# Clustered attention and MLP: the mix's second product moved from the attention into the MLP, onto gathered, turned tokens

## The chip, the cores and the metric

One NeuronCore of one Trainium2 chip runs the whole kernel. The metric is the device time of one launch in microseconds (us); the time of a version is the median of its runs. All numbers below come from the times of the version before the change and from one profiled execution of it.

## The reference, cut to what matters

The attention has 4 batches, 8 heads, 768 tokens and 64 columns per head. A query may only see keys of its own cluster. Its output, laid out as x with 768 tokens by 512 columns per batch, goes through a mix over tokens of rank 32 and an MLP:

```python
mask = q_assign[:, :, :, None] == k_assign[:, :, None, :]
scores = np.where(mask, scale * np.matmul(q, k.transpose(0, 1, 3, 2)), -1000000000.0)
attn = np.exp(scores - np.max(scores, axis=-1, keepdims=True))
attn = attn / (np.sum(attn, axis=-1, keepdims=True) + 1e-09)
x = np.matmul(attn, v)                      # then (B, S, H * D)

xt = x.transpose(0, 2, 1)
h = xt @ U @ V                              # U is 768x32, V is 32x768
u = x + h.transpose(0, 2, 1)
out = u + np.maximum(u @ w_ch1, 0.0) @ w_ch2
```

The mix of one batch is therefore u = x + Vᵀ(Uᵀx): a first product with U that needs the x of the whole batch, and a second with V, whose result is added to x.

## The kernel before, in words

**Attention.** The heads of a batch are taken in pairs, so there are 16 pairs, four to a batch. A pair goes through `rowmax` (24 matmuls of 384 columns, each followed by a DVE maximum, L421 and L423), `scores` (L445, L447, then an exponential on ACT, L450), `weights` (sums of exponentials, mostly on POOL, L460) and `values` (L468). Ahead of these stand the loads, the split of the inputs into a high and a low part, the choice of clusters on DVE (`clusters`) and several DMAs that put rows in place; `place_clusters` (L407 to L411) copies the clusters' one-hot rows `ohT`, which `rowmax` of that pair needs. `sums` (L480) makes the denominators, and `normalise` (L494 to L506) turns a pair's output back on PE and writes it, scaled, into the batch's tile `xt`: 128 partitions by 6 groups of tokens by 512 columns.

**The mix.** After a batch's last pair `mix_u` (L508) multiplies by U on PE, `mix_sum` (L523) adds the parts into `x3` (96 by 512), and `mix_v` (L531) runs six times per batch: one matmul of `x3` with a slice of `v3` (L535, 512 columns), and a DVE addition of `xt` to its result (L537). For batches 1 and 2 a DVE transpose of 32 by 32 blocks follows (L539), and `store_u` writes the batch in four DMAs (`store_blocks`, L550) to a scratch tensor `u_blk` in DRAM. Batches 0 and 3 go to `u_scr` untransposed; batch 3 is fetched back in halves inside the MLP, turned there (L753) and stored to `u_blk` (`fetch_half`, `turn_blocks`, `store_half`).

**MLP.** Batch 0 goes through two plain products (L596 to L598 and L615 to L617). Batches 1 to 3 use a scheme with seven block products instead of eight: `seven1` (L817 to L819) and `seven2` (L893 to L895), whose results `after1` and `after2` add up on DVE, and `join_up` (L931) joins into the output, after which `store` writes it. Their input is read by `fetch_columns` (L758): 16 DMAs per batch which gather pieces of 128 bytes out of `u_blk`, so that columns lie on partitions, into a tile that the trace calls `f`. `u_sums` (L773) and `u_halves` (L778, L779) work on it from there. The weights of both products go through DRAM too (`wc`); `fetch_w1` (L788) and `fetch_w2` (L800) read them back.

**The order.** Nothing is scheduled by a planner. Every step is put in a list with a time written by hand (`times`, `mixes`, `stages`, and the offsets at the end), the list is sorted, and each engine and each DMA queue runs its steps in that order. In the attention a unit of time is half a score step of a pair, 12 to a pair; in the MLP it is one step of the plain products, 32 for batch 0 and 28 for each of the others, with 24 block matmuls to a unit. Nearly all DMAs are issued by one queue, SP, which waits at the head of its line for whatever the next DMA needs. PSUM gives the work tiles (`work`, L139) four banks.

Of the kernel before, what the change touches and what calls it, by code (L numbers as in the profile page):

```python
# [59 lines left out]
    "load0":           (-34.78, -31.87, -43.69,   None,   None, -25.08),  # L60
    "load1":           (-26.31, -29.08, -32.88,   None,   None, -24.23),
    "sims":            ( -25.34, -28.59, -28.55,   None,   None, -21.62),
    "place_clusters":  (-18.26, -15.82, -15.03,   None, -10.24, -12.43),
    "split_hi0":       (-29.17, -30.78, -24.16,   None,   None, -21.89),
    "split_lo0":       (-23.33, -24.44, -23.58,   None,   None, -17.99),
    "split_hi1":       (-23.81, -23.71, -24.25,   None,   None, -18.05),
    "split_lo1":       (-23.44, -23.17, -23.57,   None,   None, -17.17),
    "place_keys_hi":   (-22.85, -23.61, -22.94,   None,   None, -17.07),
# [10 lines left out]
    "sums":            ( 14.31,  14.69,  13.43,  14.01,  15.60,  14.98),  # L79
# [3 lines left out]
    "clusters":        (-23.85, -22.92,  -23.10,   None,   None, -19.44),  # L83
# [5 lines left out]
    "mix_sum":  ( 19.29,   18.76,  19.15,  17.65),  # L89
# [6 lines left out]
    "mix":  (  3.36,   6.22,  15.04,  16.96),  # L96
    "g0":   ( 34.93,  36.17,  42.58,  52.94),
    "g1":   (-26.11, -21.73,  -20.5, -18.29),
    "g2":   (  -2.6,  -1.45,  -0.45,  -0.02,   0.14,   0.53),
# [4 lines left out]
spots = [0.22, -0.13, 1.46, 2.36, 1.94, 1.55, 2.97, 3, 3.92, 3.89, 4.51, 4.81]  # L104

# [12 lines left out]
def clustered_attention_moe(ctx: ExitStack, tc: tile.TileContext, qk, v, cen, moe_U, moe_V, w1, w2, out):  # L118
# [25 lines left out]
    u_scr = [dram.tile([P, NT, DM], F32, name=f"u_scr{b}") for b in (0, B - 1)]  # L144
    u_blk = [None, *(dram.tile([32, NT, 4, DM], F32, name=f"u_blk{b}") for b in range(1, B))]
# [152 lines left out]
    def load_mix(k, stage):  # L298
# [208 lines left out]

    def mix_u(b):  # L508
# [21 lines left out]

    def mix_v(b, t):  # L531
# [4 lines left out]
        y = x[:, t, :] if b % 3 == 0 else ps  # L536
        nc.vector.tensor_add(y, ps, x[:, t, :])  # L537
        if b % 3:
            nc.vector.transpose(x[:, t, :], ps)  # L539

    def store_u(b):
        x = live["x", b]
        if b % 3:
            store_blocks(b, 0, x)
        else:
            nc.sync.dma_start(out=u_scr[b // 3], in_=x)

    def store_blocks(b, t, x):
        for a in range(4):
            nc.sync.dma_start(out=u_blk[b][:, t:t + x.shape[1], a, :], in_=x[32 * a:32 * a + 32])  # L550
# [157 lines left out]
    def open_sevens():  # L708
# [6 lines left out]
        pool["st"] = rows.tile([P, HT, DM], F32, name="st", tag="R")  # L715
# [186 lines left out]
    def after2(b, m, e):  # L902
# [13 lines left out]
        if q:  # L916
# [249 lines left out]
```

## Time and profile before

| what | us |
|---|---|
| median of 3 runs (lowest, highest) | 964.45 (962.45, 965.26) |
| the profiled execution's own time | 962.77 |
| its span from first to last instruction | 961.0 |
| PE busy (share of the span) | 921.1 (96%) |
| DVE busy | 736.4 (77%) |
| POOL busy | 605.2 (63%) |
| ACT busy | 443.4 (46%) |
| DMA queue of SP, share of 16 engines | 70.6% |

The attention runs to about 460 us, the MLP of batch 0 to about 597 us, and the three other batches to the end. A busy PE is not PE at its peak: its matmuls are pipelined, so their listed durations overlap and a busy share of 100% can hide waits. What a step costs is read from the distance between one instruction's start and the next, from the chain of waits, and from the number of matmuls in a stretch.

### The profile page before, as it was taken

How to read it: one execution, taken by the hardware profiler on the slowest of the kernel's cores; microseconds unless marked ns; L12 is line 12 of the kernel's file. 1: busy time of each engine (PE TensorE's matmuls, PEld its weight loads, DVE VectorE, ACT ScalarE, POOL GpSimd, SP SyncE). 2: the span in 40 equal slices, each digit the busy share in tenths (PEclk: the TensorE clock that was granted, in tenths of full speed). 3: DMA queues.
4: the chain of work that ended last, by engine and by line, in shares of the span. 5: the costliest groups of instructions: out<-in, count | busy, mean ns of one | idle time of the engine just before them, and what ended most of it. 6: DMA issues, size and time to landing. Idle time of an engine off the chain costs nothing.

```text
span 961.0 us, 14990 instructions
## 1 busy us (share of the span) xinstructions
PE 921.1 (96%) x5151; PEld 757.9 (79%) x5151; DVE 736.4 (77%) x1368; ACT 443.4 (46%) x787; POOL 605.2 (63%) x448
## 2 busy tenths in 40 slices
PE   5899999999999999899999999999999999999997
PEld 2655666676656665665789999999999999999996
DVE  6798888889897787669887525867698776887776
ACT  4344555555545554357556544543335333353330
POOL 4465687899777986666165785753386543865333
PEclk9999999999999999999999999999999999999999
DMA  8584564666657563627799999789978799678634
GB/s 209 139 197 104 127 160 131 203 170 166 177 135 190 152 166 90 165 72 219 216 323 307 320 260 337 267 300 328 308 270 301 274 283 304 226 272 313 235 121 153
DMA packets 115804, 208.81 MB, mean 217 GB/s; under 512 B 46416, under 2 KB 80976, under 8 KB 111120
## 3 DMA queue, kind: packets, MB, share of 16 engines
q1 hardware_dynamic: 115344, 207.75, 70.6%
q8 instruction: 41, 0.67, 0.3%
q14 instruction: 35, 0.29, 0.1%
q10 hardware_dynamic: 384, 0.10, 0.0%
HBM read 132.64 MB, written 43.52 MB: 183 GB/s over the span
## 4 chain that ended last, share of the span: by engine, by line
PE 81%; DVE 10%; DMA 4%; issue 2%; ACT 1%; SPq 1%; POOL 0%; DVEq 0%; ACTq 0%; POOLq 0%
PE o_ps L468 13%; PE ps_max L421 7%; PE st L445 5%; PE st L447 5%; DVE m L423 3%; PE ps_p L817 3%; PE ps_p L818 3%; PE ps_p L819 3%; PE ps_q L893 3%; PE ps_q L895 3%; PE ps_q L894 3%; PE ps_q L818 3%; PE ps_q L819 3%; PE ps_q L817 3%; PE ps_h L596 2%; PE ps_h L598 2%
## 5 line engine op out<-in xcount | busy, mean ns | idle before, releaser
L460 POOL TENSOR_TENSOR T<-T,pr 128x768 f32<-128x768 f32 x120 | 223.2, 1860 | 45.1 <-ACT pr L450 16.4
L423 DVE TENSOR_REDUCE m<-ps_max 128x1 f32<-128x384 f32 x384 | 195.7, 547 | 53.1 <-PE ps_max L421 51.9
L450 ACT ACTIVATE pr<-st 128x768 f32<-128x768 f32 x192 | 155.9, 814 | 105.1 <-PE st L447 89.0
L421 PE MATMUL ps_max<-arena 128*128 128x384 f32 x384 | 124.4, 388 | 14.7 <-DMA arena<-ohT 4.6
L468 PE MATMUL o_ps<-pr,vt 128*64 128x384 f32 x768 | 132.2, 491 | 1.5 <-DVE xt L539 1.5
L421 PEld LDWEIGHTS ps_max<-arena 128*128 128x128 f32 x384 | 70.5, 195 | 60.2 <-DVE m L423 26.3
L445 PE MATMUL st<-arena 128*128 128x384 f32 x384 | 104.9, 355 | 1.9 <-ACT pr L450 1.9
L468 PEld LDWEIGHTS o_ps<-pr,vt 128*64 128x64 f32 x768 | 51.8, 136 | 66.2 <-issue 60.2
L447 PE MATMUL st<-arena 97*128 97x384 f32 x384 | 100.1, 342 | 0.6 <-DMA arena<-mT 0.4
L460 POOL TENSOR_TENSOR T<-pr 128x768 f32<-128x768 f32 x30 | 55.0, 1832 | 57.7 <-ACT pr L450 57.7
L445 PEld LDWEIGHTS st<-arena 128*128 128x128 f32 x384 | 67.4, 192 | 11.2 <-issue 6.1
L447 PEld LDWEIGHTS st<-arena 97*128 97x128 f32 x384 | 71.4, 192 | 1.6 <-DMA arena<-mT 1.1
L817 PE MATMUL ps_p<-arena,w 128*128 128x384 f32 x186 | 62.3, 335 | 0.9 <-DVE f L913 0.9
L818 PE MATMUL ps_p<-arena,w 128*128 128x384 f32 x186 | 62.2, 334 | 0.0
L819 PE MATMUL ps_p<-arena,w 128*128 128x384 f32 x186 | 62.1, 334 | 0.0
L472 ACT COPY os<-o_ps 128x384 f32<-128x384 f32 x32 | 15.4, 481 | 92.3 <-PE o_ps L468 92.3
L818 PE MATMUL ps_q<-arena,w 128*128 128x384 f32 x150 | 50.1, 334 | 0.0
L817 PE MATMUL ps_q<-arena,w 128*128 128x384 f32 x150 | 50.1, 334 | 0.0
L819 PE MATMUL ps_q<-arena,w 128*128 128x384 f32 x150 | 50.1, 334 | 0.0
L377 POOL TENSOR_TENSOR arena<-R,arena 128x768 fp32r<-128x768 f32 x18 | 36.7, 2042 | 19.0 <-ACT arena L372 13.3
L605 DVE SCALAR_TENSOR_TENSOR hx<-ps_h,hx 128x384 fp32r<-128x384 f32 x32 | 17.6, 551 | 25.4 <-ACT hx L604 25.3
L817 PEld LDWEIGHTS ps_p<-arena,w 128*128 128x128 f32 x186 | 34.9, 188 | 1.3 <-DVE f L913 1.2
(534 smaller groups left out, 2355.6 us busy)
## 6 DMA issues: line engine op xcount, KB each, us to landing
w<-wc SPq DMA_DIRECT2D x24, 1024.0 KB, 6.5
w<-wc SPq DMA_DIRECT2D x24, 768.0 KB, 5.1
arena<-wc SPq DMA_DIRECT2D x20, 768.0 KB, 9.2
rw<-in_w SPq DMA_DIRECT2D x27, 512.0 KB, 4.5
R<-in_qk SPq DMA_DIRECT2D x32, 384.0 KB, 4.6
arena<-arena SPq DMA_DIRECT2D x32, 384.0 KB, 4.8
arena<-arena SPq DMA_DIRECT2D x64, 192.0 KB, 5.3
wc<-f SPq DMA_DIRECT2D x46, 256.0 KB, 4.5
```

The lines of the kernel that those rows point to most:

```text
L377: eng.tensor_sub(part(X2[i % 3], 0, h), live["R", i][:, 2 * h:2 * h + 2].rearrange("p j q -> p (j q)"), part(X1[i % 3], 0, h))
L421: nc.tensor.matmul(ps[:, 0:HS], x1[:, 0, g // 2, g % 2, t * P:(t + 1) * P], x1[:, 1, h, g % 2, :], start=True, stop=True)
L423: nc.vector.reduce_max(live["m2", i][:, h, u:u + 1], ps[:, 0:HS], axis=AX.X)
L445: nc.tensor.matmul(st[:, j, 0:HS], x1[:, 1, hk, j, ks], x1[:, 0, h, j, :], start=True, stop=False)
L447: nc.tensor.matmul(st[:, j, 0:HS], x2[0:97, 1, hk, j, ks], x2[0:97, 0, h, j, :], start=False, stop=True)
L450: nc.scalar.activation(pr, st[:, :, 0:HS], AF.Exp, scale=SCALE)
L460: eng.tensor_add(T, live["p", i, h, 0] if c == 1 else T, live["p", i, h, c])
L468: nc.tensor.matmul(o_ps[64 * j:64 * j + 64, 0:HS], vv[:, c, j, :], pr[:, j, :], start=(c == 0), stop=(c == NT - 1))
L817: nc.tensor.matmul(ps, w[:, 0, k], u[:, 0, k], start=(k == 0), stop=False)
L818: nc.tensor.matmul(ps, w[:, 0, k], u[:, 1, k], start=False, stop=False)
L819: nc.tensor.matmul(ps, w[:, 1, k], u[:, 0, k], start=False, stop=(k == 1))
L893: nc.tensor.matmul(ps, w[:, 0], h[:, 0], start=(j == 0), stop=False)
```

## The change

For batches 1 to 3 `mix_v`, its transposes and `store_u` go. In their place:

- After each `normalise` of these batches, `turn_x` turns that pair's half (128 by 384) in blocks of 32 by 32 on DVE, and `store_x` writes it to a new scratch tensor `x_blk` on SP's queue: 24 transposes and 24 DMAs in pieces of 512 bytes.
- `x3` of each batch and `v3` are written to DRAM (`store_x3`, and one line in `load_mix`) and read back in the MLP (`load_x3`, `load_v3`) into the tile `st`, which batch 3's detour used before.
- `fetch_columns` gathers from `x_blk`, in pieces of 128 bytes as before.
- `mix_T` then makes the second product transposed, eight times per batch: one matmul of 384 columns and one DVE addition onto the gathered columns.
- Batch 3's detour (fetch, transpose, store) is gone.
- `join_up` works in halves of 384 columns, and its steps for the last batch come in another order.
- Many times in the tables move a little, and a table `shifts` moves 30 single steps.

```diff
 times = {
...
-    "place_clusters":  (-18.26, -15.82, -15.03,   None, -10.24, -12.43),
+    "place_clusters":  (-17.02, -15.82, -15.03,   None, -10.24, -12.43),
...
-    "normalise1":      ( 22.35,  16.83,  15.64,   26.38,  23.43,  19.88),
+    "normalise1":      ( 22.35,  16.83,  15.64,   27.11,  24.02,  19.88),
...
+shifts = {
+    "rowmax 14 7 0": -2.85,
...
+    "norms 1 4": 1.16,
...
+}
...
-    u_scr = [dram.tile([P, NT, DM], F32, name=f"u_scr{b}") for b in (0, B - 1)]
-    u_blk = [None, *(dram.tile([32, NT, 4, DM], F32, name=f"u_blk{b}") for b in range(1, B))]
+    u_scr = dram.tile([P, NT, DM], F32, name="u_scr")
+    x_blk = [None, *(dram.tile([NT, P, DM], F32, name=f"x_blk{b}") for b in range(1, B))]
+    x3_scr = [None, *(dram.tile([96, DM], F32, name=f"x3_scr{b}") for b in range(1, B))]
+    v3_scr = dram.tile([96, S], F32, name="v3_scr")
...
+    def turn_x(i, h):
+
+        b, p = divmod(i, NP)
+        x = live["xs", i, h] = (late if h or i == n - 1 else sb).tile([P, HS], F32, name=f"xs{h}", bufs=1,
+                                                                     tag="xs" if h or i == n - 1 else "sims")
+        nc.vector.transpose(x.rearrange("p (t d) -> p t d", t=HT),
+                            live["x", b][:, h * HT:(h + 1) * HT, p * P:(p + 1) * P])
+
+    def store_x(i, h):
+        b, p = divmod(i, NP)
+        nc.sync.dma_start(out=x_blk[b].rearrange("t q d -> q t d")[:, h * HT:(h + 1) * HT, p * P:(p + 1) * P],
+                          in_=live.pop(("xs", i, h)).rearrange("p (t d) -> p t d", t=HT))
...
-        y = x[:, t, :] if b % 3 == 0 else ps
-        nc.vector.tensor_add(y, ps, x[:, t, :])
-        if b % 3:
-            nc.vector.transpose(x[:, t, :], ps)
+        nc.vector.tensor_add(x[:, t, :], ps, x[:, t, :])
...
+    def load_x3(b):
+        nc.sync.dma_start(out=pool["st"][0:96, S:S + DM].bitcast(F32), in_=x3_scr[b])
+
+    def mix_T(b, d, h):
+
+        ps = work("ps_x")[:, 0:HS]
+        st, y = pool["st"], pool["ys"][1 - b % 2][:, d, h]
+        nc.tensor.matmul(ps, st[0:96, S + d * P:S + d * P + P], st[0:96, h * HS:(h + 1) * HS], start=True, stop=True)
+        nc.vector.tensor_add(y, ps, y)
...
-        x = u_blk[b].rearrange("r t a (d k c) -> d k r (t a) c", d=ND, k=4)[d, k]
+        x = x_blk[b].rearrange("t (a r) (d k c) -> d k r (t a) c", a=4, d=ND, k=4)[d, k]
...
-        if q:
-            for j in {B21: (1,), T2: (0, 5), T3: (3, 6), T1: (2, 4, 7)}.get(key, ()):
-                join_up(b, j)
+        for j in {B21: (1,), T2: (0, 5), T3: (3, 6, 7), T1: (4, 2)}.get(key, ()):
+            join_up(b, j, q)
...
-        eng.tensor_add(to, one, two)
+        eng.tensor_add(to[:, q], one[:, q], two[:, q])
...
+            if i >= NP:
+                at(when(f"normalise{h}", i) + 0.35, turn_x, i, h)
+                at(when(f"normalise{h}", i) + 0.9, store_x, i, h)
...
+        if b:
+            at(o + t_v, store_x3, b)
+            continue
...
-                at(o - (10, 20, 15)[b - 1] + (0.51, 0.8, 0.51)[b - 1] * k + (1.07, 3.2, 1.07)[b - 1] * d, fetch_columns, b, k, d)
+                at(o - (11.5, 20, 15)[b - 1] + (0.51, 0.8, 0.51)[b - 1] * k + (1.12, 3.25, 1.07)[b - 1] * d, fetch_columns, b, k, d)
...
+                at(o + (-8.0, -15.66, -11.2)[b - 1] + (1.0, 3.2, 1.07)[b - 1] * d + 0.3 * h, mix_T, b, d, h)
```

How the order moves is seen at three places. The first is DVE around the mix of batch 1: before, from the end of `mix_sum` on (L537 and L539 are the additions and transposes of `mix_v`, L423 the maxima of `rowmax`):

```order
L529 TENSOR_TENSOR x_2822<-ps_rep,x_2822 32x512
L423 TENSOR_REDUCE m_2554<-ps_max 128x1 x2
L537 TENSOR_TENSOR ps_h<-ps_h,xt 128x512
L539 STREAM_TRANSPOSE xt<-ps_h 128x512
L423 TENSOR_REDUCE m_2554<-ps_max 128x1 x2
L537 TENSOR_TENSOR ps_h<-ps_h,xt 128x512
L539 STREAM_TRANSPOSE xt<-ps_h 128x512
```

And with the change, from the last `normalise` of the batch on (L550 is `turn_x`, L460 the maxima, L570 and L579 belong to `mix_u` and `mix_sum`):

```order
L550 STREAM_TRANSPOSE xs_2784<-xt 128x384
L460 TENSOR_REDUCE m_2573<-ps_max 128x1
L550 STREAM_TRANSPOSE xs_2793<-xt 128x384
L460 TENSOR_REDUCE m_2573<-ps_max 128x1 x2
L570 TENSOR_TENSOR rw_g<-ps_xu,xu 128x512
L207 TENSOR_SCALAR ps_t<-rw_g 128x512
L208 SCALAR_TENSOR_TENSOR ps_t<-rw_g,ps_t 128x512
L210 SCALAR_TENSOR_TENSOR rw_t<-rw,ps_t 128x512
L579 TENSOR_TENSOR x_2847<-ps_rep,x_2847 32x512
L460 TENSOR_REDUCE m_2573<-ps_max 128x1 x4
```

The six pairs of addition and transpose that stood between the maxima after `mix_sum` are gone from there; two shorter transposes stand ahead of the mix.

The second place is SP's queue after the mix of batch 2: before, where `store_u`'s four DMAs (L550) stand ahead of a pair's row copies (L228, `ohT` being `place_clusters`):

```order
L228 DMA arena<-arena 64x1536 x2
L228 DMA arena<-arena 32x1536 x2
L550 DMA u_blk_92<-xt 192x1x512 x4
L641 DMA wc_0_99<-w_94 256x1x256
L228 DMA arena<-arena 32x1536 x2
L228 DMA arena<-ohT 32x2x384 x4
```

And with the change (L555 is `store_x`, L582 `store_x3`, L264 the row copies):

```order
L555 DMA x_blk_91<-xs_3929 128x3x128
L555 DMA x_blk_91<-xs_3933 128x3x128
L264 DMA arena<-ohT 32x2x384 x4
L582 DMA x_scr_94<-x_4003 96x512
L683 DMA wc_0_102<-w_97 256x1x256
L264 DMA arena<-arena 64x1536 x2
L264 DMA arena<-arena 32x1536 x2
L683 DMA wc_0_102<-w_97 256x1x256
L264 DMA arena<-arena 32x1536 x2
L264 DMA arena<-ohT 32x2x384 x4
```

No store of a whole batch stands ahead of the second set of `ohT` copies any more; the batch's last two stores stand ahead of the first set.

The third place is the end of DVE's order: before (L913 is `after2`, L942 `join_up`):

```order
L942 TENSOR_TENSOR acc_6181<-acc_6181 128x768
L942 TENSOR_TENSOR f<-f,acc_6181 128x2x384
L913 TENSOR_TENSOR acc<-ps_p,acc 128x384
L913 TENSOR_TENSOR acc<-ps_q,acc 128x384
L942 TENSOR_TENSOR f<-f,acc 128x2x384
L942 TENSOR_TENSOR f<-f,acc_6181 128x2x384
L913 TENSOR_TENSOR f<-ps_p,f 128x384
```

And with the change (L958 is `after2`, L986 `join_up`):

```order
L958 TENSOR_TENSOR acc_6212<-ps_q,acc_6212 128x384
L986 TENSOR_TENSOR acc_6212<-acc_6212 128x384
L986 TENSOR_TENSOR f<-f,acc_6212 128x384 x2
L958 TENSOR_TENSOR acc<-ps_p,acc 128x384
L986 TENSOR_TENSOR f<-f,acc 128x384
L958 TENSOR_TENSOR acc<-ps_q,acc 128x384
L986 TENSOR_TENSOR f<-f,acc 128x384
L958 TENSOR_TENSOR f<-ps_p,f 128x384
```

The join that stood last, between the sums of T1 and the last four additions, now comes two steps of PE earlier, and the other one is cut in halves that follow each half's sum.

## Rows read from the trace of the kernel before

**Rows 1.** The page's part 4: shares of the chain that ended last.

```profile
PE 81%; DVE 10%; DMA 4%; issue 2%; ACT 1%; SPq 1%; POOL 0%; DVEq 0%; ACTq 0%; POOLq 0%
```

**Rows 2.** By pair: stretch, its length, PE, PEld, DVE, ACT, POOL busy, clock, DMA.

```profile
121.60:145.00 23.40, 23.40 (x146) 16.05 (x146) 20.11 (x41) 12.55 (x18) 19.88 (x12) 1.00 0.60 157
145.00:174.10 29.10, 28.98 (x172) 18.60 (x171) 24.07 (x48) 14.80 (x22) 22.25 (x13) 1.00 0.51 135
...
198.70:223.50 24.80, 24.80 (x151) 17.50 (x151) 21.64 (x42) 14.54 (x21) 23.00 (x13) 1.00 0.62 165
...
247.00:279.40 32.40, 30.08 (x175) 18.57 (x177) 27.75 (x55) 14.97 (x22) 21.29 (x13) 1.00 0.51 137
279.40:305.90 26.50, 24.61 (x151) 16.86 (x153) 21.25 (x44) 13.72 (x20) 21.60 (x13) 1.00 0.73 195
...
355.30:386.40 31.10, 29.15 (x173) 18.19 (x174) 24.38 (x49) 14.16 (x21) 21.64 (x12) 1.00 0.47 119
386.40:416.10 29.70, 26.55 (x139) 18.24 (x139) 17.62 (x39) 11.03 (x16) 17.69 (x11) 0.94 0.53 133
```

**Rows 3.** The chain of waits, mix of batch 1: start, length, what.

```profile
253.19 0.99 PE ps_xu L513 x8
254.19 0.43 PE ps_xu L516 x8
...
258.64 0.63 PE ps_rep L526 x2
...
261.76 0.71 DVE ps_h L537
...
271.66 0.73 DVE xt L539
```

**Rows 4.** The chain of waits after the mix of batch 2.

```profile
400.38 2.96 DMA arena<-ohT
...
403.43 0.41 PE ps_max L421
```

**Rows 5.** SP's queue in order of time, after the mix of batch 2.

```profile
389.46 4.64 SPq L550 DMA_DIRECT2D u_blk<-xt  x4
...
398.69 2.94 SPq L228 DMA_DIRECT2D arena<-ohT  x4
```

**Rows 6.** Groups by line: busy us and mean ns; idle before.

```profile
L364 DVE STREAM_TRANSPOSE ohT<-oh 128x768 f32<-128x768 f32 x16 | 15.5, 971 | 0.1
...
L753 DVE STREAM_TRANSPOSE st<-st 128x512 f32<-128x512 f32 x6 | 4.1, 696 | 4.1 <-DMA st<-u_scr 4.1
```

**Rows 7.** The same columns for a stretch of the block products.

```profile
800.00:900.00 100.00, 100.00 (x576) 100.00 (x575) 79.36 (x140) 40.30 (x86) 60.77 (x51) 1.00 0.78 280
```

**Rows 8.** All instructions in order of time, end of the kernel.

```profile
949.11 0.96 DVE L942 TENSOR_TENSOR acc<-acc 128x768 f32<-128x768 f32 x1
...
952.14 2.54 POOL L942 TENSOR_TENSOR f<-f,acc 128x768 f32<-128x768 f32 x1 [3.05 <-DVE acc L913]
953.02 2.48 DVE L942 TENSOR_TENSOR f<-f,acc 128x768 f32<-128x768 f32 x1
...
954.45 0.33 PE L895 MATMUL ps_q<-h,arena 128*128 128x384 f32 x1
...
956.82 0.54 DVE L913 TENSOR_TENSOR f<-ps_q,f 128x384 f32<-128x384 f32 x1
```

**Rows 9.** SP's queue in order of time: gathers of batch 1.

```profile
569.52 7.75 SPq L761 DMA_DIRECT2D f<-u_blk  x6
...
583.75 0.62 SPq L761 DMA_DIRECT2D f<-u_blk  x1
```

**Rows 10.** Those gathers' landing; DVE in order of time; all engines by stretch.

```profile
DMA to landing us min/median/max: 2.7/4.6/7.1
...
580.87 0.69 DVE L669 TENSOR_TENSOR f<-ps_r,arena 128x512 f32<-128x512 f32 x1 [3.90 <-DMA wc<-f]
...
580.00:590.00 10.00, 10.00 (x50) 8.86 (x50) 7.93 (x13) 5.31 (x10) 1.42 (x2) 1.00 1.03 324
```

More of the change, by code (lines that the diff above doesn't have):

```diff
@@ L88 @@
     "mix_u":    ( 18.88,  18.35,  18.56,  16.57),
-    "mix_sum":  ( 19.29,   18.76,  19.15,  17.65),
+    "mix_sum":  ( 19.29,   18.67,  19.15,  17.65),
     "mix_v":    (  20.55,   19.49,  21.51,  18.25),
@@ L104 @@
 spots = [0.22, -0.13, 1.46, 2.36, 1.94, 1.55, 2.97, 3, 3.92, 3.89, 4.51, 4.81]
+shifts = {
+    "rowmax 14 7 0": -2.85,
+    "rowmax 0 2": -0.31,
+    "rowmax 3 9 0": 1.13,
+    "mix_T 1 3 0": 0.70,
+    "normalise 10 0": -0.37,
+    "fetch_columns 3 3 3": -0.46,
+    "rowmax 2 0 1": 2.39,
+    "clusters 1 7": 0.05,
+    "load_mix 1 2": -2.38,
+    "clusters 3 3": -0.19,
+    "scores 2 0 0": 0.47,
+    "split_lo 4 0": 1.03,
+    "seven2 3 3 6": -0.13,
+    "rowmax 2 4 0": -0.62,
+    "rowmax_place 15 0 12": -0.76,
+    "fetch_w2 6 0 3 4 5": -0.15,
+    "load_mix 0 3": 0.48,
+    "load_weights 1 6 3": 0.37,
+    "scores 9 0 0": 0.29,
+    "rowmax 0 7 0": -0.06,
+    "normalise 14 0": -1.40,
+    "recover 7 1 1 1": 0.22,
+    "load_weights 1 0 2": 1.78,
+    "scores 14 1 4": -0.74,
+    "rowmax 3 8 0": 0.26,
+    "norms 1 4": 1.16,
+    "scores 1 1 4": 0.06,
+    "turn_x 7 0": 0.24,
+    "fetch_w2 7 0 3 4 5": 0.19,
+    "rowmax 3 5 1": 0.96,
+}
 def keep_order(tc, first=0):
@@ L312, in load_mix @@
                 nc.vector.tensor_sub(v3[32:64, cols], w[32:64], v3[32:64, cols])
+                nc.sync.dma_start(out=v3_scr[:, cols], in_=v3[:, cols].bitcast(F32))
             else:
@@ L529, in mix_sum, with store_x3 @@
         nc.vector.tensor_sub(x3[64:96], ps[64:96, :], x3[64:96])
+    def store_x3(b):
+        nc.sync.dma_start(out=x3_scr[b], in_=live["x3", b].bitcast(F32))
     def mix_v(b, t):
@@ L535, in mix_v @@
         nc.tensor.matmul(ps, v3[:, t * P:(t + 1) * P], live["x3", b], start=True, stop=True)
-        y = x[:, t, :] if b % 3 == 0 else ps
-        nc.vector.tensor_add(y, ps, x[:, t, :])
-        if b % 3:
-            nc.vector.transpose(x[:, t, :], ps)
+        nc.vector.tensor_add(x[:, t, :], ps, x[:, t, :])
     def store_u(b):
[L542 to L550, printed above, removed]
+        nc.sync.dma_start(out=u_scr, in_=live["x", b])
     nh = 2
@@ L941, in join_up @@
             eng = nc.vector
-        eng.tensor_add(to, one, two)
+        eng.tensor_add(to[:, q], one[:, q], two[:, q])
         if b == B - 1:
-            for d in {1: (0, 1), 7: (2, 3)}.get(j, ()):
-                store(b, d, j == 7)
+            if j == 1:
+                store(b, q, 0)
+            if j == 4:
+                store(b, 2 + q, 1)
         elif j == 2:
-            store(b, 0)
-            store(b, 1)
+            store(b, q)
         elif j == 6:
-            store(b, 2)
-            store(b, 3)
+            store(b, 2 + q)
     M0 = NS * n + 1
@@ L959, in at @@
     def at(time, fn, *args):
-        plan.append((time, len(plan), fn, args))
+        key = " ".join(map(str, (fn.__name__, *args)))
+        plan.append((time + shifts.get(key, 0), len(plan), fn, args))
     start = [
@@ L1107, in clustered_attention_moe @@
                     at(t + U * s, seven2, b, m, e)
[L1108 removed]
+                    at(t + U * s + 0.35, after2, b, m, e)
             if which == 1:
[L1110 to L1111 removed]
+                for key, sums, high, low in ((B22, None, 1.2, 1.25), (B11, None, 1.45, 1.5), (B21, None, 1.68, 2.6),
+                                             (T3, 1.81, 2.0, 2.66), (T1, 1.95, 2.49, 3.28), (T2, 2.09, 2.3, 3.75),
                                              (T4, 2.31, 2.56, 3.41)):
@@ L1126, in clustered_attention_moe @@
             for j, when_ in enumerate((0.02, 0.79, 6.55, 6.17, 6.45, 6.35, 6.9, 6.75)):
-                at(o + 28 + when_, join_up, b, j)
+                for q in range(2):
+                    at(o + 28 + when_ + 0.12 * q, join_up, b, j, q)
     for K in range(2):
```

61 lines of the change are left out of this document (26 added, 35 removed).

## The prediction
> **What bounds the kernel now.** I read the chain that ended last first: PE holds 81% of it and DVE 10% [rows 1]. Then the stretches, because that is a mean over two very different parts. In the block products of the MLP 576 matmuls start in 100 us [rows 7], one every 0.174 us; PE has nothing to wait for there, and DVE is busy for 79% of the time. In the attention I cut the span from one pair's sums to the next pair's [rows 2]. A pair without a mix takes 23.4 to 24.8 us. The three that hold a mix take 29.1 (batch 0), 32.4 (batch 1) and 31.1 (batch 2), and two pairs behind them are long as well: 26.5 after batch 1's mix and 29.7 after batch 2's. The chain of waits says why. During batch 1's mix it runs for some 10 us on DVE, from an addition of `mix_v` at 261.8 us to the last transpose but one at 272.4 [rows 3]. After batch 2's mix it goes through the copy of the clusters' rows, which lands at 403.3 us and which PE then starts on [rows 4]. SP issued that copy from 398.7 us, behind four stores of the batch that held the queue until 394.1 [rows 5]. So in two stretches of the attention the end is set by the very steps that the change takes out; in the MLP, where it puts their replacement, it is set by the number of matmuls.
>
> **The change part by part.** The sum is made against the profiled execution, 962.77 us, which is 1.7 below the median of 964.45.
>
> *The mixes of batches 1 and 2.* Gone are 12 matmuls, 12 additions and 12 transposes. What stays is `mix_u` and `mix_sum`: 0.99 + 0.43 + 0.63 = 2.05 us of PE [rows 3]. A pair with the same weight step and no mix takes 24.8 us [rows 2], so I expect 24.8 + 2.05 = 26.85 us for each: 5.55 us less than 32.4 and 4.25 less than 31.1. A bound from below: batch 0's mix has the six matmuls and additions but no transposes and takes 29.1, which would leave 3.3 and 2.0. I take the first pair of values, since the chain runs on the additions as much as on the transposes.
>
> *The pairs behind them.* The stores of a whole batch leave SP's queue. `store_x` issues instead, and SP waits for its transpose; the loads and row copies of later pairs queue behind it. In batch 2's mix the two last stores stand ahead of a set of `ohT` copies, but their transposes are two steps behind the last `normalise`, before the mix begins, so little is held. The 26.5 goes back to 24.8: 1.7 us. Of the 29.7, up to 4.9 can go; the landing that PE waits for costs 3.0 by itself [rows 4]. I take 4.0. Late next there is the pair's own DVE work, as in any pair. These four terms make 15.5 us; their lower bounds are 3.3 + 2.0 + 0 + 3.0 = 8.3, the upper 16.4.
>
> *The 24 new transposes*, 128 by 384 from SBUF to SBUF. The trace has 0.971 us for 768 columns and 0.696 for 512 [rows 6]: 1.07 ns for a column more, so 0.56 us each and 13.4 us in all, spread over twelve pairs. How much of it reaches the end? A pair with 20.1 us of DVE work takes 23.4 us, one with 21.6 takes 24.8 [rows 2]: 0.9 us of time for one of work, if all of that is DVE's doing. It isn't: ACT has 2 us and POOL 3 us more work in the longer one. Bounds are 0 and 0.9 × 13.4 = 12; I take 0.4, nearer the lower end since DVE is never full in these pairs: 5.4 us more. The stores themselves, 24 on SP, I cost at nothing: the DMA engines are busy for 0.47 to 0.73 of these stretches [rows 2], and no one reads `x_blk` before the MLP. Writing `x3` and `v3` goes with them.
>
> *PE in the MLP.* 24 matmuls of 384 columns come in at 0.174 us [rows 7]: 4.2 us, all on the path. Batch 3's six matmuls of 512 columns, which ran inside batch 0's MLP, go: an estimate from the same row is 6 × 0.174 × 512/384 = 1.4. Net 2.8 us more. Their 24 additions take the place of 12 additions and transposes of batch 3 and have DVE's free fifth or more as cover; without it, each would hold a PSUM bank of four.
>
> *The gathers and `mix_T`.* `mix_T`'s addition waits for gathered columns, and behind it in DVE's line stand the low halves that the plain products need. A unit of the list is 24 × 0.174 = 4.2 us. In batch 1 the gathers are placed 1.5 units (6.3 us) earlier than before, and the addition for the last quarter of columns 4.7 to 5 units ahead of batch 1, at about 576 us. Before, the last gather left SP at 584.4 [rows 9]; 6.3 us earlier and 4.6 us to land [rows 10] give 582.7, some 6 us late. The low half is needed 0.7 units (2.9 us) after it is made, so PE could lose 3.5 us. But before, DVE already waited 3.9 us for a store in that stretch [rows 10], and PE, with 50 matmuls in those 10 us, lost hardly any. I take 1.0; bounds 0 and 3.5. In batches 2 and 3 two units or more lie between, so nothing. Batch 3's detour, which held SP there, is gone, and I gain nothing for it, since PE didn't wait.
>
> *The end.* PE starts its last matmul at 954.45 us, and DVE ends its last addition at 957.36 [rows 8]. In between, a join of 768 columns took 2.48 us beside one of POOL, where another took 0.96 [rows 8]. The change does that join earlier. Without the collision and the queue behind it DVE would end about 2 us sooner. But now DVE's other join, in halves, starts on the same sums as POOL's: if each half waits for one of POOL's, nothing is left. Bounds 0 and 2.0, I take 0.8. The Trainium skill, "SBUF — State Buffer", section "Who interferes with whom", has a rule that speaks against this term: a VectorE operation with both inputs in SBUF and a GpSimd operation block each other fully, whichever is second. The 2.48 beside 2.54 agrees with it, and by that rule alone the gain here would be 0 and the sum 0.8 us worse.
>
> *All other moved times* shift rows of the order by a place or two. I cost them at nothing: PE's queue of ready work covers them in the attention, as the 23.4 us pairs show.
>
> **The sum:** −15.5 + 5.4 + 2.8 + 1.0 − 0.8 = −7.1 us: 955.7 against the profiled execution, **957.3** against the median.
>
> **The rivals.**
>
> *The long pairs are long for another reason* (the weight steps on DVE that also stand in the mix, the products with U that wait for ACT). Then only the lower bounds, 8.3 us, come back, and −8.3 + 5.4 + 2.8 + 1.0 − 0.8 = 0.1: 964.5, no change. For it: batch 0's mix costs 4.3 us more than a plain pair without any transpose. Against: the chain of batch 1 names `mix_v`'s lines.
>
> *The transposes are paid in full.* Twelve pairs each grow by 1 us: −15.5 + 12 + 2.8 + 1.0 − 0.8 = −0.5: 963.9, no change. For it: the two kinds of pair in [rows 2]. Against: DVE is idle for 3 us in each.
>
> *Slower: gathers from the new layout.* In `x_blk` the pieces of one partition lie 64 KB apart, in `u_blk` 2 KB. The pieces are as many and as long, so I expect the same time. But the DMA engines are full here (1.03 between 580 and 590 us, [rows 10]), six gathers took 7.75 us to issue [rows 9], or 1.3 each, and the weights that the block products start on come behind them in the same queue. If a gather takes 1.6 times as long, 16 × 1.3 × 0.6 = 12.4 us are added ahead of batch 1, which PE waits out: 957.3 + 12.4 = 969.7. It decides from 1.5 times on. The Trainium skill, "DMA: Bandwidth & Descriptors", section "Latency and other measured facts", tells of copies that slow down when rows lie a large power of two apart, hardly at 512 KiB and clearly from 2 MiB; 64 KiB is not among its cases, and no run here shows any.
>
> *All good ends together:* −16.4 + 0 + 2.8 + 0 − 2.0 = −15.6: 948.9.
>
> That the change doesn't do what it says is excluded by the order.
>
> **How the numbers follow.** A measurement of this kernel tells some 0.3% from no change, 2.9 us: faster is below 961.6, slower above 967.3. I give the forecast (950 to 961.5) 0.58, the good ends 0.08, the first rival 0.14, the second 0.10, the third 0.10. Faster: 0.58 + 0.08 and 0.04 from the near edge of the two rivals at 964, so 0.70; same 0.19; slower 0.10 and 0.01 for both middle rivals at once, 0.11. The range runs from the good ends, 949, to the edge of the slower case, 967; outside lie half of the good ends and the slower case.
>
> **What would show it.** In the profile after: pairs with the mixes of batches 1 and 2 at about 27 us, no addition or transpose of `mix_v` in their chain, no store of a batch ahead of `ohT`; other pairs of batches 1 to 3 longer by 0.3 to 0.6 us; transposes of 0.56 us; 24 matmuls of `mix_T` at the pace of their neighbours without idle time ahead; the last addition less than 2.5 us behind the last matmul. Wrong it would be if pairs grew by 1 us or more, if PE idled near 597 us for weights or in the batch before for low halves, or if the mix pairs stayed above 29 us.

## The result and the profile after

The changed kernel takes 949.45 us (median of 5 runs, 948.59 to 950.17) beside 964.45 us of the kernel before in the same session (5 runs, 960.77 to 965.67). The ratio is 0.9855, 95% interval [0.9839, 0.9871]: faster by 1.5%. The profiled execution took 950.17 us, span 948.4, against 962.77 and 961.0: 12.6 us less. The ledger below is made between these two executions, as the prediction's sum was. (In three later sessions the median of before was 962.56, 963.52 and 963.27, so its 964.45 was a high one; the ratio of the changed kernel, run again, was 0.9859.)

The chain that ended last, from the page of after, answers to [rows 1]:

```profile
PE 83%; DVE 8%; DMA 4%; issue 2%; ACT 1%; POOL 1%; SPq 1%; ACTq 0%; DVEq 0%; POOLq 0%
```

The stretches from one pair's sums to the next pair's, in after, in the columns of [rows 2]: a plain pair with the weight step, the mix of batch 1, the pair behind it, the mix of batch 2, the pair behind it, and 100 us of block products ([rows 7]):

```profile
199.70:224.50 24.80, 24.80 (x151) 17.51 (x150) 22.49 (x44) 14.66 (x21) 23.03 (x13) 1.00 0.72 188
248.50:277.70 29.20, 27.34 (x166) 17.68 (x165) 23.77 (x46) 14.64 (x22) 22.05 (x14) 1.00 0.76 195
277.70:301.90 24.20, 24.20 (x151) 16.95 (x150) 20.65 (x43) 13.84 (x20) 21.98 (x13) 1.00 0.61 165
...
352.30:379.60 27.30, 27.07 (x170) 17.50 (x172) 20.51 (x43) 13.71 (x21) 21.19 (x12) 1.00 0.59 152
379.60:403.00 23.40, 23.18 (x138) 16.55 (x137) 16.17 (x37) 11.32 (x16) 18.24 (x11) 1.00 0.44 126
800.00:900.00 100.00, 100.00 (x577) 100.00 (x576) 80.25 (x145) 41.53 (x88) 62.00 (x56) 1.00 0.74 259
```

Read against [rows 2]: the mixes went from 32.4 to 29.2 and from 31.1 to 27.3 us, the pairs behind them from 26.5 to 24.2 and from 29.7 to 23.5. The plain pair kept its 24.8 us although DVE has 22.49 us of work in it instead of 21.64. In the last of these pairs the clock column stood at 0.94 before and is at 1.00 now. The block products are as dense as they were.

| part (profiled executions) | forecast | measured |
|---|---|---|
| two mixes and the pairs behind them | −15.5 | −15.6 (−3.2, −2.3, −3.8, −6.3) |
| other pairs (the 24 transposes) | +5.4 | +3.0 in pairs 4 to 15, +1.1 ahead of them |
| MLP of batch 0, block products (PE +2.8, gathers +1.0) | +3.8 | −0.5 and +0.9 |
| last matmul to end | −0.8 | −1.4 |
| sum | −7.1 | −12.6 |

The forecast's rows and the measured ones are not cut quite alike. Of the 24 transposes 14 start in the other pairs from pair 4 on; for these 14/24 of the 5.4, that is 3.1 us, was forecast, and 3.0 came (1.6 of it in the last interval, from pair 14's sums to pair 15's). Eight run inside the four pairs of the first row, which should therefore read −13.7, and two behind the last sums. Ahead of pair 4 no new transpose runs.

In the mix of batch 1, where [rows 3] showed a chain on DVE, after's chain waits for a load:

```profile
258.26 5.76 DMA R<-in_qk
264.06 0.84 PE ps_sim L372 x4
```

SP's queue in order of time in after, behind the mix of batch 2, answers to [rows 5]; the copies `ohT` now stand ahead of the stores, and no batch is stored:

```profile
379.18 1.62 SPq L264 DMA_DIRECT2D arena<-arena  x2
385.97 3.72 SPq L264 DMA_DIRECT2D arena<-ohT  x4
...
394.39 0.38 SPq L555 DMA_DIRECT2D x_blk<-xs  x1
```

The instructions of the tiles `xs` and `ps_x` in after (duration min/median/max in ns, first and last start), for [rows 6] and for the new matmuls and additions:

```profile
L550 DVE STREAM_TRANSPOSE xs<-xt x24: 532/568/578, 189.6 to 464.5; 128x384 f32<-128x384 f32 x24
...
L800 PE MATMUL ps_x<-st x24: 337/339/346, 553.7 to 794.3; 96*128 96x384 f32 x24
L801 DVE TENSOR_TENSOR f<-ps_x,f x24: 545/557/559, 554.1 to 794.8; 128x384 f32<-128x384 f32 x24
```

The gathers of batch 1 on SP in after, where [rows 9] had 7.75 us for six; the last leave 23 us earlier, of which the attention accounts for 12:

```profile
543.82 4.04 SPq L806 DMA_DIRECT2D f<-x_blk  x6
...
560.10 1.36 SPq L806 DMA_DIRECT2D f<-x_blk  x2
```

The end of after ([rows 8]): the joins are halves, 0.56 and 0.80 us on DVE beside two on POOL, and DVE ends its last addition at 945.19 instead of 957.36 us, 1.9 us behind the start of the last matmul instead of 2.9:

```profile
941.48 0.56 DVE L986 TENSOR_TENSOR f<-f,acc 128x384 f32<-128x384 f32 x1
...
942.54 0.80 DVE L986 TENSOR_TENSOR f<-f,acc 128x384 f32<-128x384 f32 x1
...
944.65 0.54 DVE L958 TENSOR_TENSOR f<-ps_q,f 128x384 f32<-128x384 f32 x1
...
941.59 2.61 POOL L986 TENSOR_TENSOR f<-f,acc 128x384 f32<-128x384 f32 x2 [4.21 <-DVE acc L958]
...
943.26 0.34 PE L940 MATMUL ps_q<-h,arena 128*128 128x384 f32 x1
```

### The profile page after: what moved, and what is told of

It is laid out like the page before. It is cut to its first block, busy times and chain, and to the rows that moved or that the text cites. A ratio compares the mean times of both kernels' runs of the same rounds, so it can differ in the third digit from the quotient of the medians.

```text
span 948.4 us, 15114 instructions
## 1 busy us (share of the span) xinstructions
PE 915.5 (97%) x5157; PEld 758.0 (80%) x5157; DVE 737.0 (78%) x1391; ACT 443.0 (47%) x787; POOL 608.3 (64%) x461
## 4 chain that ended last, share of the span: by engine, by line
PE 83%; DVE 8%; DMA 4%; issue 2%; ACT 1%; POOL 1%; SPq 1%; ACTq 0%; DVEq 0%; POOLq 0%
PE o_ps L505 10%; PE ps_max L458 7%; PE st L482 6%; PE st L484 5%; PE ps_p L864 3%; PE ps_p L863 3%; PE ps_p L862 3%; PE ps_q L938 3%; PE ps_q L940 3%; PE ps_q L939 3%; PE ps_q L864 3%; PE ps_q L862 3%; PE ps_q L863 3%; PE ps_p L940 3%; PE ps_p L938 3%; PE ps_p L939 3%
## 5 line engine op out<-in xcount | busy, mean ns | idle before, releaser
L460 DVE TENSOR_REDUCE m<-ps_max 128x1 f32<-128x384 f32 x384 | 194.7, 546 | 50.0 <-PE ps_max L458 48.5
L458 PE MATMUL ps_max<-arena 128*128 128x384 f32 x384 | 121.8, 383 | 7.7 <-DVE m L460 4.4
L924 POOL TENSOR_TENSOR h<-ring,h 128x384 fp32r<-128x384 f32 x17 | 17.7, 1038 | 38.6 <-ACT h L914 19.6
```

The source lines that it names most:

```text
L458: nc.tensor.matmul(ps[:, 0:HS], x1[:, 0, g // 2, g % 2, t * P:(t + 1) * P], x1[:, 1, h, g % 2, :], start=True, stop=True)
L460: nc.vector.reduce_max(live["m2", i][:, h, u:u + 1], ps[:, 0:HS], axis=AX.X)
```

## The experiments

The table has every kernel's intervals from one pair's sums to the next (pair 1 to 2, and so on; mix 1 is 7 to 8, mix 2 is 11 to 12), the start of the last pair's sums, and the ratio to before. Intervals are good to 0.1 us. An interval can differ between executions of one order: that of pair 1 is 25.5, 26.5, 26.9 and 26.4 in four that share it.

| kernel | 1–2 | 5–6 | mix 1 | behind | 9–10 | mix 2 | behind | last sums | ratio [95%] |
|---|---|---|---|---|---|---|---|---|---|
| before | 25.5 | 24.8 | 32.4 | 26.5 | 26.0 | 31.1 | 29.7 | 461.7 | 1 |
| after | 25.5 | 24.8 | 29.2 | 24.2 | 26.5 | 27.3 | 23.5 | 450.1 | 0.9855 |
| after, again | 26.5 | 24.9 | 28.2 | 24.2 | 25.3 | 27.3 | 23.5 | 448.9 | 0.9859 [0.9846, 0.9871] |
| joins in halves | 25.5 | 24.8 | 32.4 | 25.9 | 26.4 | 31.1 | 29.9 | 462.7 | 0.9967 [0.9954, 0.9979] |
| old times | 32.1 | 29.0 | 29.7 | 24.4 | 28.5 | 26.9 | 24.0 | 463.2 | 1.0008 [0.9992, 1.0024] |
| old times, stores late | 28.6 | 25.9 | 28.5 | 24.4 | 25.6 | 26.9 | 24.0 | 453.2 | 0.9951 [0.9935, 0.9966] |
| before, new times | 27.8 | 25.6 | 33.2 | 27.8 | 24.8 | 32.1 | 29.6 | 467.1 | 1.0016 [1.0003, 1.0029] |
| before, no turn | 25.5 | 24.8 | 29.0 | 28.3 | 26.2 | 28.6 | 29.7 | 457.5 | 0.9950 [0.9931, 0.9970] |
| before, copies first | 25.4 | 24.8 | 32.7 | 26.3 | 26.0 | 31.1 | 28.5 | 462.4 | 0.9992 [0.9977, 1.0007] |
| before, one store | 25.5 | 24.8 | 32.3 | 26.3 | 25.5 | 31.1 | 25.7 | 465.7 | 1.0038 [1.0023, 1.0053] |
| after, turns twice | 26.9 | 25.1 | 28.0 | 25.1 | 25.5 | 27.3 | 24.7 | 453.4 | 0.9919 [0.9907, 0.9931] |
| after, `mix_T` twice | 26.5 | 24.9 | 29.4 | 24.2 | 26.6 | 27.2 | 23.5 | 451.9 | 0.9915 [0.9902, 0.9928] |
| after, stores late | 26.9 | 24.8 | 27.5 | 24.2 | 25.6 | 27.2 | 23.5 | 447.0 | 0.9851 [0.9838, 0.9864] |
| the same, again | 26.4 | 24.9 | 27.7 | 24.2 | 25.3 | 27.2 | 23.5 | 449.1 | 0.9859 [0.9846, 0.9872] |

### The structure with the old times

```diff
-shifts = {
-    "rowmax 14 7 0": -2.85,
...
-}
+shifts = {}
-    "place_clusters":  (-17.02, -15.82, -15.03,   None, -10.24, -12.43),
+    "place_clusters":  (-18.26, -15.82, -15.03,   None, -10.24, -12.43),
-    "mix":  (  3.36,   6.22,  15.21,  18.63),
+    "mix":  (  3.36,   6.22,  15.04,  16.96),
...
```

> The whole change with the tables of times of before (all numbers that the change did not need for its new steps put back, the list of single shifts emptied). Theory (the structure, that is the mixes' second product and the single stores, carries the gain): 951 to 953 us, 10 us or more of the 15 us stay; the pairs of mix 1 and mix 2 and the pairs behind them are together still 12 to 16 us shorter than before. Rival (the gain is the re-timing's): 958 us or more, and these four pairs are together less than 8 us shorter than before.

Measured: 963.66 us, no gain at all. Neither theory had this. The four pairs of the mixes are 14.7 us shorter together (15.6 in after); but the intervals 1–2, 5–6 and 9–10 are 6.6, 4.2 and 2.5 us longer than before, and batch 0's MLP (last sums to first block product) takes 138.8 us instead of 136.9. SP's queue of this kernel shows the first of these:

```profile
92.85 0.33 SPq L318 DMA_DIRECT2D v_scr<-v  x1
93.29 1.19 SPq L233 DMA_DIRECT2D arena<-arena  x2
...
105.51 2.59 SPq L233 DMA_DIRECT2D arena<-ohT  x4
111.20 0.35 SPq L318 DMA_DIRECT2D v_scr<-v  x1
111.59 0.42 SPq L331 DMA_DIRECT2D R<-in_qk  x1
```

and the waits of SP between 86 and 112 us say for what the head of the line stood still:

```profile
SPq L318 <- DVE v L317: 19.0, 2, 16.0
```

The new store of `v3` waits up to 16.0 us for DVE, and the copies of the next pair stand behind it: `ohT` starts at 105.5 instead of 101.4 us, and the load `R` of the next pair at 111.6 instead of 104.3. The 16 us of waiting thus cost the copies 4 us and the load 7. On SP's queue in before the two stood at:

```profile
101.43 2.78 SPq L228 DMA_DIRECT2D arena<-ohT  x4
104.25 0.59 SPq L325 DMA_DIRECT2D R<-in_qk  x1
```

Here PE also lost its clock (last section).

### The old times, with the new stores later

```diff
-    "mix":  (  3.36,   6.22,  15.04,  16.96),
+    "mix":  (  3.36,   6.22,  15.21,  18.63),
...
-                at(when(f"normalise{h}", i) + 0.9, store_x, i, h)
+                at(when(f"normalise{h}", i) + ((3.5 if h else 2.2) if i < 15 else 0.9), store_x, i, h)
```

> The whole change with the tables of before, as in the earlier run (963.7 us), and two things later in the order, so that SyncE's loads and copies stand ahead of the new stores: the last two numbers of the loading of the mixes' second matrix (15.04, 16.96 become 15.21, 18.63), and each pair's stores of its turned tokens (1.3 and 2.6 steps later, but for the last pair). Theory (with the tables of before, SyncE's head waits for VectorE at the new stores, and the next pair's copies stand behind it): the interval from pair 1's sums to pair 2's goes from 32.1 us to 25 to 27 us, that from pair 5's from 29.0 to 25 to 27, that from pair 9's from 28.5 to 26 to 27.5; 951 to 956 us in all. Rival (what the re-timing moved on VectorE and TensorE is what counts, not SyncE's order): these intervals keep their length to 1 us each, 961 us or more.

Measured: 957.53 us, 0.57% of before less than without the edit (about 5.5 us; the profiled execution was 10 us shorter). The three intervals lost 3.5, 3.1 and 2.9 us. In all that is less than the theory's 951 to 956 us, and the first interval stays above its 25 to 27. In 5–6 and 9–10 PE's wait for `ohT` went from 2.4 to 0.9 and from 1.8 to 0.6 us. There it is SP's order: with the stores ahead, what they wait for is paid by the next pair. In 1–2 the edit moves the split of V on DVE as well as its store, so it doesn't tell the two apart; PE's waits for `ohT` and `R` (1.8 and 2.7 us) are gone, and it waits 2.4 us for DVE instead. The rest of the way to after, some 9 us by the ratios, lies in the other moved numbers; which of them was not tried.

### The new times alone, on the kernel before

```diff
-    "place_clusters":  (-18.26, -15.82, -15.03,   None, -10.24, -12.43),
+    "place_clusters":  (-17.02, -15.82, -15.03,   None, -10.24, -12.43),
...
-        plan.append((time, len(plan), fn, args))
+        plan.append((time + shifts.get(key, 0), len(plan), fn, args))
```

> The kernel before with the changed kernel's tables of times, its single shifts and its other numbers (but for steps that it does not have); no operation is added or left out. Theory (the re-timing only makes room for the new stores on SyncE; by itself it gains little): 960 to 964 us, the intervals of mix 1 and mix 2 and the two behind them lose under 2 us together. Rival (the re-timing is what gained): 950 to 955 us.

Measured: 964.88 us, 0.16% slower, and the four pairs some 3 us longer. The moved times are worth nothing by themselves, and the structure is worth nothing without them; together they are worth 14 us.

### The transposes of the old mix left out

```diff
-        y = x[:, t, :] if b % 3 == 0 else ps
-        nc.vector.tensor_add(y, ps, x[:, t, :])
-        if b % 3:
-            nc.vector.transpose(x[:, t, :], ps)
+        nc.vector.tensor_add(x[:, t, :], ps, x[:, t, :])
```

> The kernel before, in which the second product's 12 transposes of 0.73 us behind the mixes of batches 1 and 2 are left out (what they would turn is stored unturned), and all else is kept. Theory of the prediction (VectorE's backlog behind the mixes, 12 x 0.73 = 8.7 us in two mixes, makes these pairs and the next ones long): the four pairs together 6 to 9 us shorter, 956 to 958 us. Rival (SyncE's queue holds the next pair's loads, whatever VectorE does): the pairs that hold a mix lose 0 to 2 us together, and the pair behind mix 2, whose one-hot copies stand behind the stores on SyncE, loses 3 to 4 us only if the stores' wait for VectorE is what holds them; 960 to 963 us.

Measured: 957.70 us. The mixes lost 3.4 and 2.5 us, the pair behind mix 2 nothing, and the pair behind mix 1 grew by 1.8: 4.1 us net of the 8.7, between the two expectations. That growth is of the size of what the clock cost: this pair, in the columns of [rows 2], had 0.94 of it where before had 1.00, by an estimate 0.06 × 28.2 = 1.7 us.

```profile
275.50:303.70 28.20, 26.04 (x147) 18.18 (x146) 21.16 (x44) 13.83 (x20) 21.54 (x12) 0.94 0.71 187
```

Its chain behind mix 2 goes over a copy `ohT` that starts at 395.6 us, behind the same four stores. So the transposes lengthen the mixes, and something else lengthens the pair behind mix 2.

### The copies ahead of the stores, and one store instead of four

```diff
-    "place_clusters":  (-18.26, -15.82, -15.03,   None, -10.24, -12.43),
+    "place_clusters":  (-18.26, -15.82, -17.40,   None, -10.24, -12.43),
-    "place_queries":   (-18.82, -16.19,  -16.30,   None,   None, -16.28),
+    "place_queries":   (-18.82, -16.19,  -17.60,   None,   None, -16.28),
-    "store_u":  ( 26.55,  26.40,  26.68,  20.55),
+    "store_u":  ( 26.55,  26.40,  30.90,  20.55),
```

> The kernel before, with the copies of the one-hot rows of pair 15 (and the placing of its queries and clusters) issued on SyncE ahead of batch 2's store, and pair 12's second normalise 2.5 us later; no operation is added or left out. Theory (SyncE's queue: its head waits for VectorE's turned tokens while the copies stand behind it): the pair behind mix 2, 29.7 us before, becomes 3.0 to 3.8 us shorter, 960.5 to 962 us. Rival (VectorE's own backlog makes the pair long, the copies only show it): 0 to 1 us.

Measured: 962.36 us; the pair behind mix 2 went to 28.5, by 1.2 us only. The chain of this kernel there no longer waits for `ohT`, but for the next small copy, which now runs beside the four stores:

```profile
403.62 4.49 DMA arena<-mT
408.11 0.14 issue
408.25 0.59 PE st L447 x2
```

The 1.2 us lie just above the rival's 0 to 1, so by the expectation DVE's backlog would be the cause. But the stores were only moved here, and PE waited as long for the next copy (2.31 us) as it did for `ohT` before (2.38). What was saved is no more than the clock had cost, which stayed at 1.00 this time (last section). How much of the copy's 4.49 us the stores cause is not shown: in the kernel without the transposes the same copy took 4.52 us, more than 10 us behind the stores. Taking three of the four stores away decides whether they lengthen the pair:

```diff
-        for a in range(4):
+        for a in range(1 if b == 2 and not fill else 4):
...
+            if b == 0:
+                store_blocks(2, 0, x, True)
```

> The kernel before, in which three of the four stores of batch 2's tokens are left out (so the MLP multiplies other tokens there; that place is filled once, with four stores more, in the pair of mix 0). All of VectorE's work of mix 2 stays. Theory (the four stores' 4.64 us on SyncE, and their transfers, hold the next pair's one-hot copies, and the clock falls in that wait): the interval behind mix 2, 29.7 us, becomes 25 to 27 us. Rival (VectorE's mix work, which is late, holds them): 28.5 us or more. In all 959 to 963 us, since the filling costs up to 4 us in another pair.

Measured: the pair behind mix 2 takes 25.7 us, 4.0 less; in all 966.79 us, since the interval with the filling (4–5) went from 24.6 to 33.5, 8.9 us where up to 4 were expected. SP's queue of this kernel, to be read beside [rows 5]:

```profile
397.46 0.58 SPq L552 DMA_DIRECT2D u_blk<-xt  x1
...
402.85 3.13 SPq L228 DMA_DIRECT2D arena<-ohT  x4
```

`ohT` leaves 8.5 us behind the sums of its pair (394.4), as against 12.3 before (386.4 and 398.7). All of DVE's mix work is still there. PE doesn't wait for `ohT` any more, and its clock, in the columns of [rows 2], stays at 1.00:

```profile
402.80:406.00 3.20, 3.20 (x21) 1.35 (x18) 0.93 (x3) 0.11 (x1) 0.85 (x1) 1.00 0.34 82
406.00:410.00 4.00, 4.00 (x24) 3.68 (x24) 2.97 (x7) 2.86 (x5) 1.84 (x1) 1.00 0.88 208
```

The wait of 2.38 us in before and the 1.7 us that its clock cost (last section) make 4.1. So 4.0 of the 6.3 us are the stores'. The other 2.3, down to after's 23.5, may be what was left of the mix; no run tests that.

### The prices of the new work

```diff
-        nc.vector.transpose(x.rearrange("p (t d) -> p t d", t=HT),
-                            live["x", b][:, h * HT:(h + 1) * HT, p * P:(p + 1) * P])
+        for _ in range(2):
+            nc.vector.transpose(x.rearrange("p (t d) -> p t d", t=HT),
+                                live["x", b][:, h * HT:(h + 1) * HT, p * P:(p + 1) * P])
```

> The changed kernel with each of the 24 transposes of a pair's tokens done twice (0.57 us each, 13.6 us more of VectorE). Theory (three quarters or more of a transpose is hidden in the pairs; the first 24 cost 3 us): 952 to 955 us, 3 to 5.5 us more. Rival 1 (VectorE is behind in the pairs, a transpose is paid in full): 961 to 963 us. Rival 2 (all hidden): 949 to 950 us.

Measured: 955.24 us, 5.8 more than after's 949.45, or 0.24 for each of 24 transposes of 0.57: 43% of the work is paid. That is just above the theory's 3 to 5.5 us and far from both rivals. Of it 3.3 us had come up by the last pair's sums (4.5 against the second profile of after).

```diff
-        nc.tensor.matmul(ps, st[0:96, S + d * P:S + d * P + P], st[0:96, h * HS:(h + 1) * HS], start=True, stop=True)
+        for _ in range(2):
+            nc.tensor.matmul(ps, st[0:96, S + d * P:S + d * P + P], st[0:96, h * HS:(h + 1) * HS], start=True, stop=True)
```

> The changed kernel with each of the 24 matmuls that make the mix's second product in the MLP (339 ns, one 96x384 tile each) done twice, the second over the first. Theory of the prediction (TensorE has no gaps there, so 24 more cost 24 x 0.174 us): 4.2 us more between the first product of the blocks and the last matmul, 361 us instead of 356.7, about 953.5 us in all. Rival (part of them falls into waits that are there anyway, as the measured 0.9 us for the change says): 1 to 2 us more, 950.5 to 951.5 us.

Measured: 955.19 us against 949.76 on the same chip. Batch 0's MLP with eight of the added matmuls grew from 136.4 to 137.8 us, and the stretch of the blocks with sixteen from 357.3 (mean of after, after again and both late versions) to 359.7: 3.8 us in all, 0.16 each. They are paid nearly in full, as forecast. The blocks stay under the expected 361 because eight of the matmuls run in batch 0's MLP. In all 5.4 us were added instead of 4.2; in the profiled execution the attention was longer too (last sums at 451.9 against 448.9), though nothing was changed there.

### The joins of the last batch alone

```diff
-        if q:
-            for j in {B21: (1,), T2: (0, 5), T3: (3, 6), T1: (2, 4, 7)}.get(key, ()):
-                join_up(b, j)
+        for j in {B21: (1,), T2: (0, 5), T3: (3, 6, 7), T1: (4, 2)}.get(key, ()):
+            join_up(b, j, q)
...
-        eng.tensor_add(to, one, two)
+        eng.tensor_add(to[:, q], one[:, q], two[:, q])
...
-                at(o + 28 + when_, join_up, b, j)
+                for q in range(2):
+                    at(o + 28 + when_ + 0.12 * q, join_up, b, j, q)
```

> The kernel before with one part of the change alone: the last batch's joined sums are added and stored half by half. Theory (the last joins are the tail: with halves the last one and the stores behind it are half as long): 0.8 to 1.4 us less, all of it between the last matmul and the end of the span (6.55 us before, 5.14 us with the whole change). Rival (VectorE's and GpSimd's joins take turns, so that halves gain nothing): 0.0 us, the stretch stays at 6.5 us.

Measured: 959.59 us, 0.33% less. From the start of the last matmul to the end of the span 4.7 us are left of 6.55: 1.9 less, more than expected. The edit brings the new order of the joins along with the halves, so it doesn't say which of the two gained. The rest of the 3.2 us lies in the block products, 354.2 us here and 355.8 in before's profile; in the three experiments that left blocks and joins as before (no turn, copies first, one store) they took 354.7 to 356.8, so that part is scatter between executions.

### The stores later, in the changed kernel

```diff
-                at(when(f"normalise{h}", i) + 0.9, store_x, i, h)
+                at(when(f"normalise{h}", i) + ((3.5 if h else 2.2) if i < 15 else 0.9), store_x, i, h)
```

> The changed kernel with the pairs' stores of their turned tokens later in the order (1.3 steps for the first, 2.6 for the second, but for the last pair); in the pair that holds batch 1's mix the load of the next pair's rows then stands ahead of them on SyncE. Theory (that load, issued 258.26 and landed 5.76 us later behind the stores, ends TensorE's longest wait there): the interval of mix 1, 29.2 us, becomes 26 to 28 us; 946.5 to 948.5 us in all. Rival (the load is held by the transfers ahead of it that were there anyway): 28.5 us or more there, 949 to 950 us.

Measured: 948.54 us, the interval of mix 1 27.5. Both were run again on one chip:

> The changed kernel once more, beside the version with later stores on the same chip. Expected: 949 to 950.5 us, the interval of mix 1 29 us.

> The version with the later stores once more, beside the changed kernel on the same chip. Theory (the load of the next pair's rows no longer stands behind the stores): 1 to 3 us less than the changed kernel, the interval of mix 1 27 to 28 us. Rival (the gain seen before was another execution's): within 0.5 us of it.

Measured: 949.76 and 950.18 us, mix 1 28.2 and 27.7. PE's wait for the load, 1.3 and 0.3 us in the two profiles of after, is gone in both versions with later stores, but the total doesn't show it: the rival holds. No version here beats the changed kernel by more than its runs differ.

## Why the prediction was right, and where not

It forecast faster with 0.70 and 949 to 967 us; the median lies inside, at the fast end, and 7.9 us under the 957.3. The saving came out about twice as large as forecast: 7.1 us was forecast, 12.6 came between the profiled executions and 15.0 between the medians.

- **What bounds the kernel, and the four pairs: right in kind, the parts off.** −15.5 was forecast, −15.6 came, and the eight transposes inside are carried along. The two mixes gave 2.8 us less than forecast and the two pairs behind them 2.9 more; that this cancels is luck. Mix 1 gave 3.2 instead of 5.55, near the bound of 3.3 that batch 0's mix gave, and at 29.2 us it stayed above the 29 that the prediction named as a sign of being wrong (28.2 in the second profile). In part that is the late load `R`: with the stores later it took 27.5 and 27.7, still more than 26.85. The pair behind mix 2 gave 6.3 instead of 4.0. That term, put together from the landing of one copy, lacked the clock (below), worth 1.7 us in 403.4 to 408.5, and took "up to 4.9" for the whole of what can go. The plain pairs vary more than "23.4 to 24.8" says: 1–2 takes 25.5 and 9–10 takes 26.0 in before.
- **"The stores themselves, 24 on SP, I cost at nothing … Writing x3 and v3 goes with them", and "All other moved times … I cost them at nothing": both failed.** With the old times three intervals grew by 13.3 us, nearly the 14.7 that the four pairs gain (963.66 us in all); with the stores later 9.5 of them came back. The moved times take the loss back. The two errors have opposite signs and nearly cancelled, so it is luck that the sum came out with the right sign. The stores were costed by the DMA engines' share; what they take is the head of SP's line. The rest of the 14 us is not taken apart.
- **The transposes: size right.** 0.568 us against 0.56. The factor 0.4 was picked between two bounds; doubling them gave 0.43, and the 14 transposes of the ledger 0.38 (3.0 of 14 × 0.568). Full payment (the second rival) falls. One pair did grow by more than the 1 us that was to show the prediction wrong: from pair 14's sums to pair 15's, 1.6 us (0.9 in the second profile).
- **PE in the MLP: price right, sum too high.** 0.16 for a matmul against 0.174. Yet batch 0's MLP and the blocks took 0.4 us more together instead of the 3.8 forecast with the gathers. Part of it is before's profiled execution: its blocks took 355.8, those of the four experiments on before that kept its tables 354.2 to 356.8 (mean 355.1), those of after, after again and both late versions 356.7 to 358.4 (mean 357.3), so the blocks' share is nearer 2.
- **The gathers: 1.0 forecast, nothing seen.** The longest of DVE's waits between 550 and 590 us in after name `mix_T`'s matmuls (9.5 us in six), none names a gather, and no wait of PE is listed there. The last gathers left 11 us earlier than the shorter attention accounts for, where 6.3 were forecast. Six gathers issue in 4.04 us instead of 7.75, and the transfers of 128 bytes took 13 ns each in both traces, so the slower rival, which wanted 1.6 times as long a gather, falls. The Trainium skill ("DMA: Bandwidth & Descriptors", "Latency and other measured facts") measured slower copies where the rows of different partitions lie a large power of two apart; here the 64 KB lie between the pieces of one partition, and the 13 ns show no harm.
- **The end: mis-sized.** 0.8 forecast, 1.4 in after, 1.9 alone. It was held down by "if each half waits for one of POOL's, nothing is left". DVE's second half took 0.80 us instead of 0.56, so beside POOL's it lost 0.24 us, where the whole join had lost 1.52 (2.48 instead of 0.96). The Trainium skill ("SBUF — State Buffer", "Who interferes with whom") calls the port pair that the two engines share an exclusive lock. The trace agrees: the four halves end in turn, DVE at 942.04, POOL at 942.92, DVE at 943.34, POOL at 944.20 us, and POOL's two take 1.3 us each where one alone takes 1.0. So the rule stands, but "the gain here would be 0" did not follow from it: in halves, what one engine waits for is shorter.
- **The first rival** (long for another reason) falls: leaving out the transposes shortened the mixes by 3.4 and 2.5 us, and leaving out three stores the pair behind by 4.0, with all else in place.

## What to carry to other kernels

Cost a new DMA first by what it makes its queue wait for: a store of a few tenths of a microsecond that needs a late engine's result holds every load behind it; here that came to nearly as much as the four pairs gain. So a new structure and the order written for the old one are measured together: here each alone was worth nothing and both 14 us. And a stall that a step causes is not gone when the step is moved past one copy: here PE then waited as long for the next one.

## What the runs showed of the hardware that was not expected

A wait of PE costs more than its length when the granted clock falls behind it. The stretches of before around the wait for `ohT` that [rows 4] showed, in the columns of [rows 2]:

```profile
399.00:403.40 4.40, 2.04 (x11) 1.51 (x10) 1.48 (x4) 2.44 (x3) 3.23 (x2) 1.00 0.86 232
403.40:408.50 5.10, 5.07 (x23) 4.90 (x23) 3.16 (x7) 1.38 (x3) 3.90 (x3) 0.67 0.75 228
408.50:414.00 5.50, 5.38 (x31) 2.49 (x30) 1.86 (x4) 1.41 (x3) 1.98 (x2) 1.00 0.00 0
```

PE idled for 2.38 us and then had 0.67 of its clock for 5.1 us, some of that time at 1.2 instead of 2.4 GHz: by an estimate 0.33 × 5.1 = 1.7 us on top. The kernel with the old times shows it twice, after 2.40 us of idle time (0.67) and, between the sums of pairs 1 and 2, after 1.82 and 2.67 us (0.61):

```profile
115.00:119.40 4.40, 4.16 (x15) 3.06 (x16) 0.56 (x1) 0.81 (x1) 1.50 (x1) 0.61 0.17 68
...
219.90:225.00 5.10, 5.10 (x27) 3.93 (x27) 3.31 (x7) 1.81 (x3) 3.92 (x3) 0.67 0.52 136
```

After 2.31 us of idle time with the copies first, and after 1.31 us in mix 1 of after, it stayed at 1.00. So two waits of nearly the same length, 2.38 and 2.31 us, differed by some 1.7 us in what they cost; what decides between them is not shown.
